# Attention and two expert layers on one core: weights of the second layer decoded once into float32, and the last block's products in another order

## The chip, the cores and the metric

The kernel runs on one core of one Trainium2 chip. The metric is the time of one execution on the device in microseconds; three runs of the kernel before are given, and one more execution was recorded by the hardware profiler.

## What is computed

The reference, cut to its core (shapes: 8 batches, 8 heads, 576 positions, head size 64; so 4608 tokens of width 512):

```
scores = q_c @ k_c.T / sqrt(64)              # in chunks of 64 positions
attn   = softmax(scores)
x      = (attn @ v_c)  as [4608, 512]
a, b   = x @ w1, x @ w2                       # [512, 1024] each
x      = ((a * b) @ w3) @ w_out               # [1024, 1024], [1024, 512]
h      = x @ w_in                             # [512, 2048]
out    = (h * cos(h)) @ w_out2                # [2048, 512]
```

The weights arrive as float64, each word pair of which the kernel turns into one float32 by itself.

## The kernel before, in words

The tokens are cut into 9 blocks of 512. Three kinds of matmul work follow each other for a block: attention (four tiles of 128 tokens, lines 724 to 787), the products a and b (ab, line 1000), and u, the product with w3 @ w_out folded into one matrix (lines 1110 to 1112). u is written to DRAM (line 1124). When all blocks are through, a second phase reads u back block by block and does h = u @ w_in (line 1318), cosine, and y = g @ w_out (line 1418). Every product of ab, h and y is a Strassen-Winograd product of seven terms on halves; each float32 operand is split into two float16 parts, so a term is three matmuls per piece. Three PSUM banks, x, y and z, collect the seven terms: ACT copies a bank out (`kept`), DVE adds another bank to what was copied (`plus`), and a term that continues in a bank (`more`) waits until the copy before it has been made.

Nothing in this kernel is issued in the order of the source. Each operation is recorded with an engine, a cost and a due time, and the class `Plan` lists them: at each moment every engine takes the waiting operation with the earliest due time whose buffers are free. The due times come from one line of constants (line 300). A2 and A3 set when the four attention tiles of a block are due ahead of its ab, I0 to I5 when the weights of the second layer are prepared, and Y0, Y1, YU when the terms of y and their weights are due. All loads and stores but one kind go through SP's queue, which is in order: an entry that waits holds up what stands behind it. The exception are additions of h operands by POOL's accumulating DMA (line 1348).

The second layer's weights are prepared while the blocks' ab and u run. `survey` (w_in first, w_out later) loads 16 pieces of 128 x 512 float64 each and takes the largest magnitude of each by a DVE reduction (line 584). From the maximum comes a power-of-two scale (`scale_of`). Then `convert_in` and `convert_out` load the same pieces a second time. `decoded` turns each into float32 in place (one ACT operation, line 1166; three on DVE, lines 1169, 1172, 1175), which leaves the values in every second word. Sums and differences for the Strassen terms are made in the words between (line 1246 on DVE or POOL for w_in, line 1202 on DVE for w_out). Each operand is split in two float16 parts by ACT (lines 1261, 1218) and DVE (lines 1264, 1221) and stored to `win_dram` and `wout_dram` (lines 1267, 1225). The second phase fetches them from there for every block (lines 1275, 1283).

`y_of` for the last block uses banks x, y, z as for every other: terms 0 (x), 1 (y), 5 (z), 4 (x), 3 (x), 2 with weight 6 (z), and 6 with weight 2 (x). The last store to the output is line 1445.

Of the kernel before, what the change touches and what calls it, by code (L numbers as in the profile page):

```python
# [262 lines left out]
def fused_kernel(  # L263
# [36 lines left out]
    R0, R1, C0, C1, A0, A1, A2, A3, R2, RL, C2, W0, X0, I0, I1, I2, I3, I4, I5, F0, Y1, Y0, YU = 2.0, 9.7, 15.9, 27.4, 89.8, 11.4, 70.0, 10.6, 47.7, 4.0, 74.1, -0.1, 14.0, 260.0, 10.0, 28.1, 410.0, 5.6, 11.6, 8.4, 16.0, 8.0, 9.05  # L300
# [79 lines left out]
    )  # L380
    two_p = sbuf_pool(one_half, *line("CONV", 24 * KB, 2 * KB, 4))
# [80 lines left out]
    with tc.manual_schedule():  # L462
# [619 lines left out]
        def u_scales(first, last, prio):  # L1082
# [4 lines left out]
            (b, t), c = small([P, 3, m], f"hsc{first}"), 2.0 ** (TOP - 2) / DM  # L1087
# [70 lines left out]
        def decoded(at, j, n, pool):  # L1158

            raw = load_raw(at, piece_of(j, n), "raw", pool)  # L1160
            def low():
                return raw.ap[:, :, 0]
            def high():
                return raw.ap[:, :, 1]
            def f():
                nc.scalar.activation(high().bitcast(F32), high().bitcast(F32), AF.Copy, scale=2.0**-112)
            op("ACT", 0.67, at - 2, f, r=[raw], w=[(raw, 1)])
            def f():
                nc.vector.tensor_scalar(low(), low(), 29, None, ALU.logical_shift_right)
# [12 lines left out]
        def convert_out(prio, step):
# [8 lines left out]
            def side(raw, n, h):  # L1191
                return raw.ap[:, 256 * h : 256 * h + 256, n].bitcast(F32)

            for kt in range(8):
                at = prio + 2 * step * kt
                top, low = (decoded(at + i * step, 1, kt + 8 * i, raw2_p) for i in range(2))
                at += step
                b11, b12, b21, b22 = ((raw, 0, h) for raw in (top, low) for h in range(2))
                t1, t3, t2, t4 = ((raw, 1, h) for raw in (top, low) for h in range(2))
# [8 lines left out]
                for i, (raw, n, os, m) in enumerate(((top, 0, slice(0, 1), 0), (low, 0, slice(1, 3), 0), (top, 1, slice(3, 6, 2), 0), (low, 1, slice(4, 7, 2), 1))):  # L1208
# [6 lines left out]
                    def val(raw=raw, n=n, width=width):  # L1215
                        return raw.ap[:, :width, n].bitcast(F32).rearrange("p (o e) -> p o e", e=256)
# [317 lines left out]
```

## Time and profile before

| what | us |
|---|---|
| runs of the kernel before, median (lowest to highest of 3) | 1413.06 (1412.48 to 1414.01) |
| the profiled execution, own time | 1407.62 |
| its span, first to last instruction | 1405.4 |
| PE busy in the span | 1367.8 (97%) |
| DVE, ACT, POOL busy | 1169.8, 961.3, 233.4 |

The page shows for each engine the time in which an instruction of it ran. PE is TensorE's matmuls. Idle time of PE is put down to the engine whose semaphore came last. The granted clock of TensorE is at its upper level, 2.4 GHz, from 50 to 1400 us.

### The profile page before, as it was taken

Reading aid. Unit: us, or ns where it says so; the run is one execution under the profiler, and the core shown is the slowest. Engines: PE = TensorE matmul, PEld = TensorE weight load, DVE = VectorE, ACT = ScalarE, POOL = GpSimd, SP = SyncE. Lnnn points to the kernel's source line nnn. Section 1 sums busy time; section 2 is a strip of 40 time slices with the busy share of each in tenths; the row PEclk is TensorE's granted clock in tenths of the full one; section 3 lists DMA queues with packets and bytes.
Section 4 is the critical chain, followed back from the end, with each engine's and each line's share of the span. In section 5 each row is a group of like instructions: output and inputs, shape, how many; then the busy total and the mean of one; then the engine's idle time right before and its main releaser. Section 6 shows DMA issues by size and latency. Waiting matters only on the chain.

```text
span 1405.4 us, 32143 instructions
## 1 busy us (share of the span) xinstructions
PE 1367.8 (97%) x12984; PEld 1103.3 (79%) x12984; DVE 1169.8 (83%) x2014; ACT 961.3 (68%) x2098; POOL 233.4 (17%) x198
## 2 busy tenths in 40 slices
PE   8889999999999999999999999999999999999998
PEld 5447677868676777786877888888888888888887
DVE  7999887448897878984669999999999898988883
ACT  5987786769886769885557666675656565755651
POOL 0000124113643212332111010000010011010000
PEclk9999999999999999999999999999999999999999
DMA  9962582236669528541625888778887878787634
GB/s 286 307 142 46 168 275 52 71 76 175 162 182 294 167 69 233 158 135 31 241 76 175 260 245 274 261 243 260 267 255 233 286 244 269 241 267 240 239 124 148
DMA packets 196628, 276.81 MB, mean 197 GB/s; under 512 B 121216, under 2 KB 151936, under 8 KB 187264
## 3 DMA queue, kind: packets, MB, share of 16 engines
q1 hardware_dynamic: 187264, 257.99, 57.5%
q0 software_dynamic: 9216, 16.78, 6.8%
q8 instruction: 101, 1.65, 0.5%
q14 instruction: 47, 0.39, 0.1%
HBM read 224.40 MB, written 33.55 MB: 184 GB/s over the span
## 4 chain that ended last, share of the span: by engine, by line
PE 71%; DVE 17%; DMA 5%; ACT 4%; issue 2%; SPq 1%; ACTq 0%; DVEq 0%; POOLq 0%
PE ps L1000 19%; PE ps L1418 18%; PE ps L1318 16%; PE ps L1110 4%; PE ps L1112 4%; PE ps L1111 4%; DVE W L1342 3%; DVE RES L1361 2%; DMA WG<-in_moe_w_dram 2%; PE ps L724 2%; PE ps L787 1%; PE ps L739 1%; DVE RES L1358 1%; DMA ATT<-in_v_dram 1%; DVE W L896 1%
## 5 line engine op out<-in xcount | busy, mean ns | idle before, releaser
L1000 PE MATMUL ps<-XHL,W 128*128 128x256 f16 x3024 | 349.2, 273 | 6.6 <-ACT RES L490 4.2
L1318 PEld LDWEIGHTS <-ATT 128*128 128x128 f16 x3024 | 295.7, 98 | 42.7 <-issue 6.9
L1000 PEld LDWEIGHTS <-W 128*128 128x128 f16 x3024 | 292.3, 98 | 46.8 <-issue 8.7
L1418 PE MATMUL ps<-CONV,W 128*128 128x256 f16 x2352 | 278.0, 273 | 1.7 <-ACT CONV L1433 1.6
L1418 PEld LDWEIGHTS <-W 128*128 128x128 f16 x2352 | 230.0, 98 | 29.2 <-issue 2.2
L1318 PE MATMUL ps<-XHL,ATT 128*128 128x256 f16 x1536 | 190.6, 273 | 2.1 <-DVE XHL L667 1.5
L1364 ACT ACTIVATE RES<-RES,quarter 128x512 f32<-128x512 f32 x144 | 103.4, 718 | 99.8 <-DVE RES L1361 99.5
L490 ACT ACTIVATE RES<-ps,smalls 128x512 f32<-128x512 f32 x126 | 86.7, 696 | 44.8 <-PE ps L1000 41.6
L1020 DVE SCALAR_TENSOR_TENSOR RES<-ps,smalls,RES 128x512 f32<-128x512 f32 x108 | 79.6, 745 | 41.3 <-ACT RES L490 27.3
L1110 PE MATMUL ps<-WG 128*128 128x512 f16 x288 | 109.3, 379 | 0.2 <-DVE RES L1070 0.2
L1112 PE MATMUL ps<-WG 128*128 128x512 f16 x288 | 109.2, 379 | 0.0
L1111 PE MATMUL ps<-WG 128*128 128x512 f16 x288 | 109.2, 379 | 0.0
L1035 POOL TENSOR_TENSOR WG<-RES,WG 128x512 f16<-128x512 f32 x49 | 63.0, 1291 | 271.1 <-ACT WG L486 271.0
L756 ACT ACTIVATE ATT<-ps,SMALL 128x64 f32<-128x64 f32 x288 | 85.7, 326 | 29.2 <-DVE SMALL L751 24.1
L1318 PE MATMUL ps<-WG,ATT 128*128 128x256 f16 x768 | 94.1, 273 | 1.2 <-DVE WG L1333 0.4
L1318 PE MATMUL ps<-RES,ATT 128*128 128x256 f16 x720 | 89.1, 273 | 2.4 <-ACT WG L1327 2.4
L1339 ACT ACTIVATE W<-WG,smalls 128x512 f16<-128x512 f32 x102 | 71.8, 714 | 22.7 <-DVE WG L1352 9.7
L1418 PE MATMUL ps<-CONV,WG 128*128 128x256 f16 x672 | 81.7, 273 | 0.0
L1342 DVE SCALAR_TENSOR_TENSOR W<-WG,smalls,W 128x512 f16<-128x512 f32 x102 | 74.8, 746 | 2.6 <-ACT W L1339 2.4
L667 DVE SCALAR_TENSOR_TENSOR XHL<-XHL,smalls 128x512 f16<-128x512 f32 x80 | 65.3, 838 | 10.7 <-ACT XHL L664 10.5
L486 ACT COPY ATT<-ps 128x512 f32<-128x512 f32 x108 | 61.3, 593 | 18.6 <-PE ps L724 9.6
L1348 POOL DMA_DIRECT2D WG<-WG x30 | 26.8, 893 | 277.7 <-DVE WG L1352 84.1
(211 smaller groups left out, 2395.8 us busy)
## 6 DMA issues: line engine op xcount, KB each, us to landing
ATT<-win_dram SPq DMA_DIRECT2D x72, 896.0 KB, 6.9
CONV<-wout_dram SPq DMA_DIRECT2D x63, 1024.0 KB, 6.1
CONV<-in_moe_w_in_dram SPq DMA_DIRECT2D x32, 512.0 KB, 6.2
CONV<-in_moe_w_out_dram SPq DMA_DIRECT2D x32, 512.0 KB, 6.1
ATT<-in_v_dram SPq DMA_DIRECT2D x144, 64.0 KB, 3.1
u_dram<-TMP SPq DMA_DIRECT2D x36, 256.0 KB, 3.7
XHL<-u_dram SPq DMA_DIRECT2D x9, 1024.0 KB, 8.2
out_dram<-CONV SPq DMA_DIRECT2D x36, 256.0 KB, 5.4
```

What stands on the lines that cost most here:

```text
L490: nc.scalar.activation(dst, src, AF.Copy, scale=s)
L756: nc.scalar.activation(probs()[:, b, a], scores()[:, a, b], AF.Exp, scale=scale, bias=mb.ap[:, 1, a, b : b + 1], accum_out=zb.ap[:, b, a : ...
L1000: nc.tensor.matmul(ps.ap[:, p * half : (p + 1) * half], w12[j, g].ap[:, b, w_, c, p * P : (p + 1) * P], t[a].ap[:, c, u_], start=(not more ...
L1020: nc.vector.scalar_tensor_tensor(b.ap, ps.ap, inv[1], b.ap, ALU.mult, ALU.add)
L1110: nc.tensor.matmul(ps.ap, wh.ap[:, kk, 0, ns], g[:, 0], start=(kk == 0), stop=False)
L1111: nc.tensor.matmul(ps.ap, wh.ap[:, kk, 0, ns], g[:, 1], start=False, stop=False)
L1112: nc.tensor.matmul(ps.ap, wh.ap[:, kk, 1, ns], g[:, 0], start=False, stop=(kk == K1 - 1))
L1318: nc.tensor.matmul(ps.ap[:, p * half : (p + 1) * half], wins[p].ap[:, b, k, w_], t[a].ap[:, k, u_], start=(not more and p == 0 and k == 0 ...
L1339: nc.scalar.activation(d.ap[:, 0], hs.ap, AF.Copy, scale=sg[1])
L1342: nc.vector.scalar_tensor_tensor(d.ap[:, 1], hs.ap, sg[1], d.ap[:, 0], ALU.mult, ALU.subtract)
L1364: nc.scalar.activation(r.ap, r.ap, AF.Sin, bias=quarters[side], scale=(2 * side - 1) * TURN)
L1418: nc.tensor.matmul(ps.ap[:, j * 256 : (j + 1) * 256], g[:, u_, n, j * P : (j + 1) * P], w.ap[:, 2 * f_ + n, w_], start=(not more and f_ == ...
```

## The change

Five things are done. `survey` decodes each piece, once, into float32, takes the sum of its squares on ACT instead of a maximum on DVE, and stores the 256 KB to a new DRAM tensor `dec_dram`; the scale comes from the sum (`sum_of`, `root_of`). `decoded` now only loads 256 KB of float32 from there. The differences for w_in are made in place, on DVE alone, and their operands read adjacent words. The last block's terms run in the order 0, 1, 5, 4, 2, 3, 6, where term 2 goes to bank y and term 6 to two banks of h, one for each half of its rows, each half added and stored by itself. And constants change: A2, A3, I0, I2, I3, I4, Y0, Y1, YU (F0 is read nowhere).

```diff
-    R0, R1, C0, C1, A0, A1, A2, A3, R2, RL, C2, W0, X0, I0, I1, I2, I3, I4, I5, F0, Y1, Y0, YU = 2.0, 9.7, 15.9, 27.4, 89.8, 11.4, 70.0, 10.6, 47.7, 4.0, 74.1, -0.1, 14.0, 260.0, 10.0, 28.1, 410.0, 5.6, 11.6, 8.4, 16.0, 8.0, 9.05
+    R0, R1, C0, C1, A0, A1, A2, A3, R2, RL, C2, W0, X0, I0, I1, I2, I3, I4, I5, F0, Y1, Y0, YU = 2.0, 9.7, 15.9, 27.4, 89.8, 11.4, 65.0, 7.2, 47.7, 4.0, 74.1, -0.1, 14.0, 241.9, 10.0, 34.8, 416.4, 5.7, 11.6, 7.2, 16.4, 10.3, 8.8
...
+    dec_p = sbuf_pool(plain, *line("CONV", 24 * KB, 2 * KB, 4))
+    piece_p = sbuf_pool(plain, *line("CONV", 0, 2 * KB, 12), queue=True)
...
-            (b, t), c = small([P, 3, m], f"hsc{first}"), 2.0 ** (TOP - 2) / DM
+            (b, t), c = small([P, 3, m], f"hsc{first}"), 2.0 ** (TOP - 2)
...
+        dec_dram = dram.tile([2, 16, P, 512], F32, name="dec_dram")
+        kept_f = Buf(None, "dec_dram")
+
         def survey(j, prio, step):
 
-            pm = small([P, 16], f"pmi{j}")
+            pm = small([P, 1, 16], f"pmi{j}")
             for n in range(16):
-                raw = load_raw(prio + step * n, piece_of(j, n), "look", raw2_p)
-                def f(raw=raw, n=n):
-                    absmax(pm[1][:, n : n + 1], raw.ap[:, :, 1].bitcast(F32))
-                op("DVE", 0.69, prio + step * n, f, r=[raw], w=[(pm[0], n)])
-            b, t = small([P, 16], f"wm{j}")
-            def f():
-                nc.vector.tensor_scalar(t, pm[1], 2.0**-112, None, ALU.mult)
-                nc.vector.tensor_scalar(t.bitcast(U32), t.bitcast(U32), 3, None, ALU.logical_shift_left)
-            op("DVE", 0.35, prio + 16 * step, f, r=[(pm[0], n) for n in range(16)], w=[b])
-            wsc[j] = scale_of(prio + 16 * step, b, t, f"wio{j}")
+                at = prio + step * n
+                raw, c = load_raw(at, piece_of(j, n), "raw", raw2_p), Buf(dec_p, f"dec{j}_{n}")
+                def low(raw=raw):
+                    return raw.ap[:, :, 0]
+                def high(raw=raw):
+                    return raw.ap[:, :, 1]
+                def f(high=high):
+                    nc.scalar.activation(high().bitcast(F32), high().bitcast(F32), AF.Copy, scale=2.0**-112)
+                op("ACT", 0.67, at - 2, f, r=[raw], w=[(raw, 1)])
+                def f(low=low):
+                    nc.vector.tensor_scalar(low(), low(), 29, None, ALU.logical_shift_right)
+                op("DVE", 0.45, at, f, r=[(raw, 0)], w=[(raw, 0)])
+                def f(low=low, high=high):
+                    nc.vector.scalar_tensor_tensor(low(), high(), 3, low(), ALU.logical_shift_left, ALU.bitwise_or)
+                op("DVE", 0.78, at, f, r=[(raw, 0), (raw, 1)], w=[(raw, 0)])
+                def f(low=low, high=high, c=c):
+                    nc.vector.scalar_tensor_tensor(c.ap.bitcast(U32), high(), SIGN, low(), ALU.bitwise_and, ALU.bitwise_or)
+                op("DVE", 0.7, at, f, r=[(raw, 1), (raw, 0)], w=[c])
+                def f(c=c, n=n):
+                    squares(pm[1][:, 0, n : n + 1], junk, c.ap)
+                op("ACT", 0.7, at + 1, f, r=[c], w=[(pm[0], n)])
+                def f(c=c, n=n):
+                    nc.sync.dma_start(dec_dram[j, n], c.ap)
+                op("SP", 0.6, at + 1, f, r=[c], w=[(kept_f, (j, n))], size=P * 2 * KB)
+            q = sum_of(prio + 16 * step, pm[0], range(16), pm[1], f"wm{j}")
+            wsc[j] = root_of(prio + 16 * step, *q, f"wio{j}")
...
         def decoded(at, j, n, pool):
+            raw = Buf(pool, f"piece{j}_{n}")
+            def f():
+                nc.sync.dma_start(raw.ap, dec_dram[j, n])
+            op("SP", 0.6, at - 10, f, r=[(kept_f, (j, n))], w=[raw], size=P * 2 * KB)
...
+                        def f():
+                            nc.vector.tensor_tensor(out=value(out), in0=value(x), in1=value(y), op=ALU.subtract)
+                        op("DVE", 0.7, at, f, r=[x, y, out], w=[out])
+                    def goes(o, raw, i):
+                        four_parts(at + i * step / 14, raw, (fb, fs), o, k, c)
+                    goes(0, b11, 0)
+                    sub(b12, b11, b11)
+                    sub(b22, b12, b12)
+                    goes(2, b22, 1)
+                    goes(1, b21, 2)
+                    sub(b22, b11, b22)
+                    goes(3, b11, 3)
+                    sub(b21, b22, b21)
+                    goes(5, b12, 4)
+                    goes(4, b22, 5)
+                    goes(6, b21, 6)
...
+            if last:
+                m4 = Buf(ps_y["y"], "psy4")
+                m3 = [Buf(ps_h, f"psy3_{j}") for j in range(2)]
+                multiply(x, 4, 4, 3, True)
+                c21 = kept(x, "u2", 3)
+                plus(z, c21, 3)
+                multiply(m4, 2, 6, 4)
+                plus(m4, c21, 4)
+                store(c21, 1, 0, 4)
+                multiply(x, 3, 3, 5, True)
+                c22, c12 = kept(x, "v5", 5), kept(x, "v3", 5)
+                plus(z, c22, 5)
+                store(c22, 1, 1, 5)
+                w = fetch(bl, 2, prio + 6 * unit - Y1)
+                for j in range(2):
+                    def f(j=j):
+                        for f_ in range(4):
+                            g = tg[6, f_].ap.rearrange("p s (f t) -> p s f t", f=2)
+                            for n in range(2):
+                                for m, (u_, w_) in enumerate(((0, 0), (1, 0), (0, 1))):
+                                    nc.tensor.matmul(
+                                        m3[j].ap[:, :256], g[:, u_, n, j * P : (j + 1) * P], w.ap[:, 2 * f_ + n, w_],
+                                        start=(f_ == 0 and n == 0 and m == 0), stop=(f_ == 3 and n == 1 and m == 2),
+                                    )
+                    op("PE", 12 * MM, prio + 6 * unit + j, f, r=[tg[6, f_] for f_ in range(4)] + [w], w=[m3[j]])
+                    def f(j=j):
+                        nc.vector.scalar_tensor_tensor(c12.ap[:, j], m3[j].ap[:, :256], iy[1], c12.ap[:, j], ALU.mult, ALU.add)
+                    op("DVE", 0.4, prio + 6 * unit + j, f, r=[m3[j], iy[0], c12], w=[(c12, j)])
+                    def f(j=j):
+                        nc.sync.dma_start(out[bl * T + j * P : bl * T + (j + 1) * P, 256:], c12.ap[:, j])
+                    op("SP", 0.6, prio + 6 * unit + j, f, r=[(c12, j)], size=P * KB)
+                return
```

The order of the instructions follows from the plan, so here are two places of it. Line numbers in the changed kernel are higher: L1138 is the raw load L1136 of before, L1126 the store of u, L642 and L719 the loads of v and of q and k.

SP's queue where the survey of w_in begins, before:

```order
L640 DMA ATT<-in_v_dram 64x4x64 x4
L717 DMA ATT<-in_k_dram 128x8x64
L1136 DMA CONV<-in_moe_w_in_dram 128x1024 x12
L1124 DMA u_dram<-TMP 128x512
L640 DMA ATT<-in_v_dram 64x4x64 x4
L1136 DMA CONV<-in_moe_w_in_dram 128x1024 x4
L1124 DMA u_dram<-TMP 128x512 x2
```

and from the middle of that survey on in the changed kernel (L1174 is the new store):

```order
L719 DMA ATT<-in_k_dram 128x8x64
L1138 DMA CONV<-in_moe_w_in_dram 128x1024
L1174 DMA dec_dram<-CONV 128x512
L1138 DMA CONV<-in_moe_w_in_dram 128x1024
L1126 DMA u_dram<-TMP 128x512
L1138 DMA CONV<-in_moe_w_in_dram 128x1024
L1174 DMA dec_dram<-CONV 128x512 x2
L1126 DMA u_dram<-TMP 128x512 x2
L1138 DMA CONV<-in_moe_w_in_dram 128x1024
L1174 DMA dec_dram<-CONV 128x512
```

The burst of raw loads is gone; loads now alternate with stores that wait for DVE, and the stores of u stand among them.

DVE's last rows, before (L1439 is `plus`):

```order
L1342 SCALAR_TENSOR_TENSOR WG<-RES,smalls,WG 128x512
L1342 SCALAR_TENSOR_TENSOR W_67<-W_67,smalls 128x512 x3
L1439 SCALAR_TENSOR_TENSOR CONV<-ps_77,smalls,CONV 128x512
L1439 SCALAR_TENSOR_TENSOR CONV<-ps_78,smalls,CONV 128x512 x2
```

and in the changed kernel (L1457 is `plus`, L1498 the addition of one half):

```order
L1457 SCALAR_TENSOR_TENSOR CONV<-ps_78,smalls,CONV 128x512
L1457 SCALAR_TENSOR_TENSOR CONV<-ps_77,smalls,CONV 128x512
L1457 SCALAR_TENSOR_TENSOR CONV<-ps_78,smalls,CONV 128x512
L1498 SCALAR_TENSOR_TENSOR CONV<-ps_76,smalls,CONV 128x256
L1498 SCALAR_TENSOR_TENSOR CONV<-ps_75,smalls,CONV 128x256
```

The last work behind PE moves from ACT's copy of a whole bank to DVE's addition of a half.

## Rows read from the trace of the kernel before

**Rows 1.** The page of the whole kernel: span, and busy time of each engine
```profile
span 1405.4 us, 32143 instructions
PE 1367.8 (97%) x12984; PEld 1103.3 (79%) x12984; DVE 1169.8 (83%) x2014; ACT 961.3 (68%) x2098; POOL 233.4 (17%) x198
```

**Rows 2.** Windows by stage: busy us (instructions) of each engine, granted clock, DMA share, GB/s
```profile
325.00:425.00 100.00, 97.99 (x1053) 77.22 (x1053) 91.01 (x131) 85.28 (x231) 51.80 (x34) 1.00 0.63 171
425.00:500.00 75.00, 71.70 (x789) 53.70 (x787) 58.38 (x109) 54.45 (x153) 23.34 (x19) 1.00 0.73 222
650.00:725.00 75.00, 74.26 (x604) 53.66 (x603) 42.49 (x77) 36.79 (x77) 14.33 (x10) 1.00 0.33 122
725.00:800.00 75.00, 72.98 (x619) 59.99 (x617) 71.05 (x126) 54.16 (x88) 7.19 (x8) 1.00 0.65 200
800.00:875.00 75.00, 74.19 (x678) 66.01 (x676) 73.94 (x122) 48.26 (x76) 7.73 (x9) 1.00 0.85 276
875.00:950.00 75.00, 71.98 (x658) 64.06 (x656) 72.14 (x119) 49.21 (x77) 6.11 (x7) 1.00 0.78 247
950.00:1375.00 425.00, 425.00 (x3896) 380.87 (x3894) 384.33 (x623) 259.41 (x398) 36.23 (x40) 1.00 0.77 243
```

**Rows 3.** Waits of PE, 375 to 500 us: total us, times, longest us
```profile
PE ps L1000 <- ACT RES L490: 3.0, 2, 1.5
PE ps L739 <- ACT ATT L756: 1.4, 1, 1.4
```

**Rows 4.** Waits of PE, 640 to 930 us
```profile
PE ps L1318 <- ACT WG L1327: 2.7, 2, 2.4
PE ps L1318 <- DVE XHL L667: 1.5, 1, 1.5
PE ps L1318 <- DVE WG L1333: 1.1, 2, 0.7
```

**Rows 5.** Waits of ACT, 888 to 927 us
```profile
ACT W L1339 <- DMA RES<-W: 3.2, 1, 3.2
```

**Rows 6.** Timeline of the end: start us, us, instruction [idle before, releaser]
```profile
1384.02 0.69 ACT L1433 ACTIVATE CONV<-ps,smalls 128x512 f32<-128x512 f32 x1 [6.79 <-PE ps L1418]
1384.76 5.40 PE L1418 MATMUL ps<-CONV,W 128*128 128x256 f16 x48 [0.78 <-ACT CONV L1433]
1390.93 10.64 PE L1418 MATMUL ps<-CONV,W 128*128 128x256 f16 x96 [0.78 <-ACT CONV L1433]
1401.66 0.69 ACT L1433 ACTIVATE CONV<-ps,smalls 128x512 f32<-128x512 f32 x1 [10.78 <-PE ps L1418]
```

**Rows 7.** DMA issues, 1401 to 1406 us: KB each, median us from issue to landing
```profile
out_dram<-CONV SPq DMA_DIRECT2D x1, 256.0 KB, 2.1
```

**Rows 8.** Groups of instructions by form: busy us, mean ns | idle before
```profile
L570 ACT ACTIVATE junk<-XHL 128x512 bf16<-128x512 f32 x36 | 22.7, 630 | 1.1
L570 ACT ACTIVATION_READ_ACCUMULATOR junk<-XHL 128x1 f32 x36 | 6.7, 186 | 0.0
L584 DVE TENSOR_REDUCE smalls<-CONV 128x1 f32<-128x512 f32 x32 | 21.2, 681 | 12.3 <-DMA CONV<-in_moe_w_out_dram 11.7 <-DMA CONV<-in_moe_w_in_dram 0.6
L1172 DVE SCALAR_TENSOR_TENSOR CONV<-CONV 128x512 uint32<-128x512 uint32 x32 | 31.6, 987 | 1.4
L1367 DVE TENSOR_TENSOR WG<-WG,RES 128x512 f32<-128x512 f32 x76 | 51.9, 685 | 4.9 <-ACT RES L1364 4.7
L1202 DVE TENSOR_TENSOR CONV<-CONV 128x256 f32<-128x256 f32 x32 | 14.8, 483 | 0.2
L1246 POOL TENSOR_TENSOR CONV<-CONV 128x512 f32<-128x512 f32 x13 | 22.5, 1733 | 15.7 <-DVE CONV L1175 12.7 <-DVE SMALL L763 1.4 <-PE ps L724 1.3
```

**Rows 9.** DMA issues of the whole kernel, from the page
```profile
CONV<-in_moe_w_in_dram SPq DMA_DIRECT2D x32, 512.0 KB, 6.2
```

**Rows 10.** Waits of SP's DMA queue, 170 to 700 us
```profile
SPq L1267 <- DVE CONV L1264: 25.6, 12, 7.2
```

**Rows 11.** Waits of PE, 0 to 100 us
```profile
PE ps L724 <- DMA ATT<-in_q_dram: 2.5, 1, 2.5
```

More of the change, by code (lines that the diff above doesn't have):

```diff
@@ L1182, in convert_out, with value @@
+        def value(raw):
+            return raw.ap
         def convert_out(prio, step):
@@ L1189, in convert_out, with halves, side @@
             op("DVE", 0.3, prio, f, r=[bs], w=[fb])
-            def side(raw, n, h):
-                return raw.ap[:, 256 * h : 256 * h + 256, n].bitcast(F32)
+            def halves(raw, width):
+                return [(raw, h) for h in range(width // 256)]
+            def side(raw, h):
+                return raw.ap[:, 256 * h : 256 * h + 256]
             for kt in range(8):
                 at = prio + 2 * step * kt
-                top, low = (decoded(at + i * step, 1, kt + 8 * i, raw2_p) for i in range(2))
+                top, low = (decoded(at + i * step, 1, kt + 8 * i, piece_p) for i in range(2))
                 at += step
-                b11, b12, b21, b22 = ((raw, 0, h) for raw in (top, low) for h in range(2))
-                t1, t3, t2, t4 = ((raw, 1, h) for raw in (top, low) for h in range(2))
+                more = [Buf(piece_p, f"sums{kt}_{i}") for i in range(2)]
+                b11, b12, b21, b22 = ((raw, h) for raw in (top, low) for h in range(2))
+                t1, t3, t2, t4 = ((raw, h) for raw in more for h in range(2))
                 def sub(x, y, out, how=ALU.subtract):
@@ L1202, in f @@
                         nc.vector.tensor_tensor(out=side(*out), in0=side(*x), in1=side(*y), op=how)
-                    op("DVE", 0.4, at, f, r=[x[:2], y[:2]], w=[out[:2]])
+                    op("DVE", 0.4, at, f, r=[x, y], w=[out])
                 sub(b11, b12, t1)
@@ L1207, in convert_out @@
                 sub(b21, t2, t4)
-                for i, (raw, n, os, m) in enumerate(((top, 0, slice(0, 1), 0), (low, 0, slice(1, 3), 0), (top, 1, slice(3, 6, 2), 0), (low, 1, slice(4, 7, 2), 1))):
+                for i, (raw, os, m) in enumerate(((top, slice(0, 1), 0), (low, slice(1, 3), 0), (more[0], slice(3, 6, 2), 0), (more[1], slice(4, 7, 2), 1))):
                     dst, width = Buf(two4_p, f"wo{kt}_{i}"), 256 if i == 0 else 512
@@ L1240, in convert_in, with four_parts @@
                     at = prio + step * (2 * k + c)
-                    b11, b12, b21, b22 = (decoded(at + i * step / 8, 0, 4 * (k + 2 * (i // 2)) + c + 2 * (i % 2), raw2_p) for i in range(4))
+                    b11, b12, b21, b22 = (decoded(at + i * step / 8, 0, 4 * (k + 2 * (i // 2)) + c + 2 * (i % 2), piece_p) for i in range(4))
                     at += step / 2
                     def sub(x, y, out):
-                        def f(eng):
-                            engines[eng].tensor_tensor(out=value(out, 1), in0=value(*x), in1=value(*y), op=ALU.subtract)
-                        op(TT, 0, at, f, r=[x, y], w=[(out, 1)])
-                    sub((b12, 0), (b11, 0), b11)
-                    sub((b22, 0), (b11, 1), b22)
-                    sub((b22, 0), (b12, 0), b12)
-                    sub((b21, 0), (b22, 1), b21)
-                    for o, (raw, n) in enumerate(((b11, 0), (b21, 0), (b22, 0), (b11, 1), (b22, 1), (b12, 1), (b21, 1))):
-                        four_parts(at + o * step / 14, raw, n, (fb, fs), o, k, c)
-        def four_parts(at, raw, n, scale, o, k, c):
+                        def f():
[14 more added lines that the diff above has]
+                    goes(6, b21, 6)
+        def four_parts(at, raw, scale, o, k, c):
             dst = Buf(two4_p, f"wi{o}_{k}{c}")
```

36 lines of the change are left out of this document (9 added, 27 removed).

## Prediction

> **What bounds the kernel.** I read the page first: PE is busy in 1367.8 of 1405.4 us [rows 1], so all that any change of order can give back is the 37.6 us in which PE stood idle. The number of matmuls hardly changes (two small transposes and their followers go, two small sums come), so a gain must come out of idle time, and the windows by stage tell where that lies. From 325 to 500 us PE lacks 2.01 and 3.30 us, from 650 to 725 us 0.74, and in the first part of the second phase, 725 to 950 us, 2.02, 0.81 and 3.02 us [rows 2]. From 950 to 1375 us nothing is lost: 425.00 of 425.00 [rows 2]. So the long second phase cannot be made faster by this change at all, whatever it does to other engines there. These six windows hold 11.9 us and the end 5.4 (below); the other 20.3 us lie elsewhere, nearly all ahead of 325 us, where the first weights are made and the change leaves the work alone.
>
> The waits of PE then say what ended the idle time. From 375 to 500 us it is ACT: 3.0 us for the copy out of a bank (L490) and 1.4 us for an exponential of attention (L756) [rows 3]. From 640 to 930 us it is again ACT's copy (2.7 us), the float16 parts of u (1.5 us) and `plus` (1.1 us) [rows 4]. The largest of these, 2.4 us, comes after ACT has stood 3.2 us at the head of its queue for an accumulating DMA that landed late [rows 4, 5]. At the end there are two waits of 0.78 us each for a copy of bank x, and after the last matmul (1390.93 + 10.64 = 1401.57 us) another 3.83 us until the span ends [rows 6].
>
> **The last block's terms.** Before, term 3 is added in bank x directly behind term 4, so PE waits 0.78 us for the copy, and the next term waits 0.78 us for the copy of term 3 [rows 6]. Now term 2 goes to bank y and stands between terms 4 and 3; it takes 48 matmuls, which last 5.40 us, and the copy it hides lasts 0.69 us [rows 6]. Term 6 goes to two banks of h that nothing uses any more, so nothing is waited for there either. Both waits go: **-1.56 us**. If the cover were gone, the same 0.78 us each would be back; no third wait is late next, since the last weights have two whole terms, some 10.6 us, to land [rows 6].
>
> **The last store.** Before, ACT copies a bank of 128 x 512 in 0.69 us [rows 6], and 256 KB need 2.1 us from issue to landing [rows 7]. Now DVE adds 128 x 256; the nearest row of that size took 483 ns [rows 8]: -0.2 us. The store has 128 KB left. Its landing lies between 2.1 us (no gain) and half of that, 1.05 us; no row has this size at an idle queue. I take 1.7 us, -0.4, since part of a landing is there for any size. Together **-0.6 us**, with ends of -0.2 and -1.25. [...]
>
> **Preparing w_in and w_out.** What goes on DVE: 32 maxima of 681 ns, 21.8 us [rows 8]. The three decoding operations per piece are moved to the survey, not removed. What comes on ACT: 32 squares at 630 ns and, behind each, a read of the accumulator at 186 ns, 20.2 us at least and 26.1 us if nothing overlaps [rows 8]. POOL loses its 13 differences, 22.5 us at 1733 ns each, and DVE takes them at some 685 ns, +8.9 us [rows 8]. One decoding operation took 987 ns on average where a float32 operation of the same size takes 685 ns [rows 8]; with POOL off these tiles and the converting reads adjacent, up to 0.3 us of each such operation may go, 9.7 us for 32. So DVE loses 12.9 to 22.6 us and ACT gains 20 to 26 us.
>
> In bytes nothing changes: 32 second loads of 512 KB (half of the 32 of w_in [rows 9] and as many of w_out) make 16.8 MB, and 32 stores and 32 loads of 256 KB make 16.8 MB. But SP issues 32 entries more, and each store waits for DVE.
>
> All of this lies beside PE's work, so by itself I cost it at nothing. The cover on ACT is its idle time: it is busy 85.28 of 100 us from 325 to 425, and 54.45 of 75 us from 425 to 500 [rows 2]; one survey adds 10 to 13 us, which would fill the fuller window to about 98. If that cover goes, the copies out of the banks come late, and PE pays as in [rows 3]. DVE at 91.01 of 100 us [rows 2] gets lighter, though, and ACT's exponentials and copies wait on DVE's operations about as often as the reverse.
>
> **The constants.** A block's last attention tile is due at 70 - 3 x 10.6 = 38.2 us ahead of its ab before, and at 65 - 3 x 7.2 = 43.4 us now: 5.2 us more lead for the operands of ab, and the tiles closer together. Both waits of [rows 3] stand where a block's ab begins while exponentials of the next tiles fill ACT's queue. I take half of the 5.31 + 0.74 us of these stages [rows 2] as saved: **-3.0 us**. The ends are -6.05 (all of it) and +6 (as much again, if ACT's added squares do there what the exponentials do now).
>
> For the second phase Y0 + i x YU moves term 0 by +2.3 us and term 6 by +0.8 us, with weights asked for 0.4 us earlier. This shuffles which operation stands in front of which between 725 and 950 us, where DVE is busy 71 to 74 of 75 us [rows 2] and has no slack to repair a late DMA. There 5.85 us are lost, about half of it behind one late landing [rows 5]. An order that is another one need not repeat it, and may have its own: I take **-1.0 us**, between -5.85 and +3.0 (one more such landing).
>
> **The sum.** -1.56 - 0.6 - 3.0 - 1.0 = -6.2 us. The profiled execution took 1407.62 us by its own time, 2.2 more than its span, and would come to 1401.4. The runs shown have a median of 1413.06, 0.4% above the profiled one; the difference goes onto the median: 1406.9 us.
>
> **Rivals.** *Only the end is gained.* The plan deals out the same PE work against nearly the same sums of other engines; a wait removed at one block's start can reappear at another's. Then -1.56 - 0.6 is what is left, 1410.9 us. For it speaks that PE's idle time in the middle stages is only 6.05 us in all, so that little noise eats a part of it; against it, that both ends of the tiles' schedule move the right way.
>
> *All idle time of these stages goes.* -2.2 - 6.05 - 5.85 = -14.1, or 1399.0 us. Against it: six stages would have to be clean where each lost something before [rows 2].
>
> *SP's queue holds up attention: slower.* The 32 added stores each wait on SP until DVE has decoded a piece. Stores of the like (L1267) were held 25.6 us over 12 waits, 2.1 us each, 7.2 at most [rows 10]. Behind them in the queue stand loads of q, k, v and the stores of u, as the order of SP's rows shows. Loads of q and k are asked for 12 units ahead of use (line 717), so the rival decides once about six mean holds fall in a row. PE's price for one late load of q was 2.5 us [rows 11]; at three blocks' starts that is +7.5, with the end -2.2: +5.3, or 1418.4 us. Against it: the loads in the burst that was there before are gone, and in the survey's windows DMA is busy 0.63 to 0.73 of the time [rows 2]. The Trainium skill's page "DMA: Bandwidth & Descriptors", section "Anatomy of one DMA", says that DMA engines do not wait for semaphores and that the issuing sequencer does so before dispatch; by that rule a held store delays all that SP issues later, and the trace agrees: SP's own waits are listed as such [rows 10].
>
> *The change doesn't do what it says.* If pieces were still read as float64 the second time, nothing would move in the stage. The order shows loads of 128 x 512 from `dec_dram`, so this has 0.02, at 1413.
>
> **How the numbers follow.** A measurement of this kernel can tell about 0.2%, 2.8 us, from no change. Forecast (-3 to -10): 0.48. All goes: 0.10. Only the end, -2.2, inside 0.2%: 0.25. No effect: 0.02. Slower: 0.15. So faster by over 0.2% 0.58, within 0.27, slower 0.15. The range reaches from 1400.0 (the forecast's -6.2 with most of the remaining idle time gone) to 1414.5 (only the end, with a new wait of some 3.6 us); outside are half of the second rival and nearly all of the slower one, some 0.18.
>
> **What would show it.** In the changed kernel's trace: no wait of PE for L1433's successor in the last block, and under 3.5 us from the last matmul to the end; no maxima on DVE, 32 squares on ACT; PE's waits for ACT's copies between 200 and 725 us at about 3 us in all; some 5 us of idle PE from 725 to 950 us. It would be wrong if PE's waits name q, k or v loads or ACT's copies for over 6 us between 200 and 725 us, or if the start of the second phase loses as much as before or more.

## The result, and the profile after

| what | before | after |
|---|---|---|
| median of 4 runs, us (lowest to highest) | 1412.77 (1411.77 to 1414.01) | 1401.35 (1400.49 to 1401.85) |
| ratio of the runs, 95% interval | | 0.9918 [0.9901, 0.9935] |
| recorded execution, own time and span, us | 1407.62, 1405.4 | 1401.22, 1398.8 |

The change saves 11.4 us by the medians, but only 6.4 us between the two recorded executions. Before was recorded 5.2 us below its median, after 0.1 us. That gap makes up nearly half of the saving.

The changed kernel's page, for [rows 1]:

```profile
span 1398.8 us, 32260 instructions
PE 1365.6 (98%) x12977; PEld 1102.3 (79%) x12982; DVE 1153.0 (82%) x1994; ACT 974.4 (70%) x2162; POOL 206.5 (15%) x183
```

DVE lost 16.8 us, ACT gained 13.1 and POOL lost 26.9. PE's idle time fell from 37.6 to 33.2 us. The windows by stage of the changed kernel (busy us and instructions of PE, weight loads, DVE, ACT, POOL; granted clock, DMA share, GB/s), for [rows 2]:

```profile
325.00:425.00 100.00, 96.14 (x1062) 75.47 (x1060) 86.27 (x140) 87.05 (x237) 33.73 (x25) 1.00 0.84 244
425.00:500.00 75.00, 75.00 (x822) 57.19 (x821) 48.13 (x93) 56.50 (x172) 16.22 (x13) 1.00 0.36 98
650.00:725.00 75.00, 75.00 (x613) 54.60 (x612) 44.55 (x76) 34.69 (x62) 16.69 (x12) 1.00 0.29 108
725.00:800.00 75.00, 72.95 (x619) 60.10 (x617) 71.25 (x126) 54.58 (x89) 7.22 (x8) 1.00 0.65 200
800.00:875.00 75.00, 74.31 (x680) 66.30 (x678) 74.21 (x124) 49.75 (x78) 8.08 (x9) 1.00 0.85 271
875.00:950.00 75.00, 74.69 (x685) 66.77 (x684) 71.79 (x117) 49.44 (x78) 7.24 (x8) 1.00 0.79 255
950.00:1375.00 425.00, 425.00 (x3895) 380.94 (x3894) 387.63 (x628) 257.67 (x397) 34.88 (x39) 1.00 0.75 243
```

From 425 to 500 us nothing is lost any more (3.30 before), from 875 to 950 us 0.31 (3.02 before). From 325 to 425 us the loss grew from 2.01 to 3.86 us, at a DMA share of 0.84 where it was 0.63. PE's waits of the changed kernel from 640 to 930 us (total us, times, longest), for [rows 4]:

```profile
PE ps L1336 <- DVE XHL L669: 1.4, 1, 1.4
PE ps L1336 <- DVE WG L1351: 1.0, 2, 0.7
PE ps L1336 <- ACT WG L1345: 0.4, 1, 0.4
PE ps L1336 <- DMA ATT<-win_dram: 0.3, 1, 0.3
```

The 2.7 us behind ACT's copy are down to 0.4. The end of the changed kernel's timeline (start us, us, instruction, idle before), for [rows 6]:

```profile
1375.80 14.14 PE L1436 MATMUL ps<-CONV,W 128*128 128x256 f16 x128
...
1389.77 5.40 PE L1492 MATMUL ps<-CONV,W 128*128 128x256 f16 x48
1389.97 1.27 ACT L1451 ACTIVATE CONV<-ps,smalls 128x512 f32<-128x512 f32 x2 [9.79 <-PE ps L1436]
...
1395.21 0.48 DVE L1498 SCALAR_TENSOR_TENSOR CONV<-ps,smalls,CONV 128x256 f32<-128x256 f32 x1 [2.07 <-PE ps L1492]
```

No row of PE has an idle time before it: both waits of 0.78 us are gone. The last matmul ends at 1395.17 us, 3.63 us ahead of the span's end (3.83 before). The groups by form that answer to [rows 8]:

```profile
L572 ACT ACTIVATE junk<-CONV 128x512 bf16<-128x512 f32 x32 | 20.8, 650 | 0.6 <-DVE CONV L1168 0.3
L572 ACT ACTIVATION_READ_ACCUMULATOR junk<-CONV 128x1 f32 x32 | 6.9, 215 | 0.0
L1168 DVE SCALAR_TENSOR_TENSOR CONV<-CONV 128x512 uint32<-128x512 uint32 x32 | 29.5, 922 | 0.6
L1213 DVE TENSOR_TENSOR CONV<-CONV 128x256 f32<-128x256 f32 x32 | 18.9, 625 | 0.2
L1257 DVE TENSOR_TENSOR CONV<-CONV 128x512 f32<-128x512 f32 x16 | 13.3, 831 | 0.3
```

The squares cost 27.7 us on ACT. A decoding operation fell from 987 to 922 ns. The sums of w_out rose from 483 to 625 ns each; in e9, where they read the same words as before, they take 651 ns, so the new layout needn't be the cause. The 16 differences on DVE take 831 ns each.

### The profile page after: what moved, and what is told of

Its sections match the earlier page's. It is cut to its first block, busy times and chain, and to the rows that moved or that the text cites. A ratio compares the mean times of both kernels' runs of the same rounds, so it can differ in the third digit from the quotient of the medians.

```text
span 1398.8 us, 32260 instructions
## 1 busy us (share of the span) xinstructions
PE 1365.6 (98%) x12977; PEld 1102.3 (79%) x12982; DVE 1153.0 (82%) x1994; ACT 974.4 (70%) x2162; POOL 206.5 (15%) x183
## 4 chain that ended last, share of the span: by engine, by line
PE 74%; DVE 15%; ACT 4%; DMA 4%; issue 2%; SPq 1%; POOL 0%; ACTq 0%; DVEq 0%
PE ps L1002 20%; PE ps L1436 19%; PE ps L1336 17%; PE ps L1112 4%; PE ps L1113 4%; PE ps L1114 4%; DVE W L1360 3%; PE ps L726 2%; PE ps L950 2%; DVE RES L1379 1%; PE ps L789 1%; PE ps L741 1%; DVE RES L1376 1%; DMA CONV<-in_moe_w_out_dram 1%; DVE XHL L669 1%
## 5 line engine op out<-in xcount | busy, mean ns | idle before, releaser
L1436 PE MATMUL ps<-CONV,W 128*128 128x256 f16 x2304 | 273.4, 273 | 0.0
L1357 ACT ACTIVATE W<-WG,smalls 128x512 f16<-128x512 f32 x101 | 71.3, 713 | 25.0 <-DVE WG L1385 12.6
L1345 ACT ACTIVATE WG<-ps,smalls 128x512 f32<-128x512 f32 x76 | 51.0, 680 | 48.5 <-PE ps L1336 47.9
L669 DVE SCALAR_TENSOR_TENSOR XHL<-XHL,smalls 128x512 f16<-128x512 f32 x81 | 68.5, 863 | 9.0 <-ACT XHL L666 8.9
L1360 DVE SCALAR_TENSOR_TENSOR W<-WG,smalls,W 128x512 f16<-128x512 f32 x101 | 74.1, 745 | 0.9 <-ACT W L1357 0.8
L1436 PEld LDWEIGHTS <-WG 128*128 128x128 f16 x672 | 65.8, 98 | 7.6
```

The source lines that it names most:

```text
L669: nc.vector.scalar_tensor_tensor(d.ap[:, :, 1], ap(x), scale[1], d.ap[:, :, 0], ALU.mult, ALU.subtract)
L1360: nc.vector.scalar_tensor_tensor(d.ap[:, 1], hs.ap, sg[1], d.ap[:, 0], ALU.mult, ALU.subtract)
L1436: nc.tensor.matmul(ps.ap[:, j * 256 : (j + 1) * 256], g[:, u_, n, j * P : (j + 1) * P], w.ap[:, 2 * f_ + n, w_], start=(not more and f_ == ...
```

## The experiments

The idle time below is worked out from each kernel's windows by stage: the width less PE's busy time. L584 waits are DVE's waits for raw pieces at the survey's maxima from 425 to 500 us. The last column is the time from 200 to 1375 us in which the granted clock stood at its lower level, 1.2 GHz. PE counts as busy there, but its matmuls start at half the rate (e1's rows below), so up to half of that time is lost on top of the idle time. One execution of each kernel was recorded, so a microsecond between two rows can be chance; the ratios come from 4 to 12 runs each, and e1 to e4, e5 to e8 and e9 to e12 ran on one chip each, beside runs of before.

| kernel | ratio to before [95%] | PE idle 200 to 725 | 725 to 950 | 950 to 1375 | L584 waits | at 1.2 GHz |
|---|---|---|---|---|---|---|
| before | 1 | 6.05 | 5.85 | 0 | 11.7 | 0 |
| e1, before again | 1.0002 [0.9991, 1.0014] | 7.31 | 5.30 | 0.85 | 13.1 | 6.8 |
| e2, last block only | 0.9984 [0.9971, 0.9997] | 7.60 | 4.24 | 1.57 | 12.5 | 0 |
| e3, constants only | 0.9945 [0.9927, 0.9963] | 4.00 | 3.73 | 0 | 5.4 | 6.8 |
| e4, decoding only | 0.9945 [0.9929, 0.9962] | 4.14 | 4.47 | 0 | none | 6.8 |
| after | 0.9918 [0.9901, 0.9935] | 4.42 | 3.05 | 0 | none | 0 |
| e5, after, old A2, A3 | 0.9960 [0.9946, 0.9974] | 3.54 | 6.62 | 0.35 | none | 3.4 |
| e6, after, old Y | 0.9945 [0.9925, 0.9964] | 2.94 | 4.73 | 0 | none | 0 |
| e7, after, old I | 0.9919 [0.9905, 0.9934] | 2.27 | 3.19 | 0.51 | none | 0 |
| e8, after, nudged | 0.9940 [0.9921, 0.9960] | 3.43 | 4.66 | 0 | none | 0 |
| e9, before, no survey of w_out | 0.9963 [0.9948, 0.9977] | 7.10 | 3.77 | 0 | none | 3.4 |
| e10, after, squares twice | 0.9899 [0.9882, 0.9916] | 4.50 | 3.99 | 0 | none | 0 |
| e11, after, one last store | 0.9912 [0.9897, 0.9928] | 3.60 | 3.06 | 0.09 | none | 0 |
| e12, after, later surveys | 0.9894 [0.9876, 0.9912] | 3.05 | 3.14 | 0.26 | none | 3.4 |

### The kernel before once more, and each part alone

**Before again** has no edit; it shows how two recordings of one program differ.

> The kernel before, unchanged, with a profile of its own. The recorded execution of before took 1407.6 us while its other runs took 1411.8 to 1414.0; the changed kernel's recorded execution (1401.2) lies among its other runs. Theory A (the trace that I read shows before as it mostly runs): a new recorded execution comes out within 2 us of 1407.6 again or of 1412.8, and shows the same idle stretches of PE. Theory B (before has a wait whose length varies from run to run, by some 5 us, which the trace I read had at its short end): a new trace shows one or two idle stretches of PE that are longer than in the first, most likely at a late accumulating DMA or a late load between 375 and 925 us, with the rest equal.

It was recorded at 1414.96 us, 7.3 us above the first recording, as Theory B had it: PE has a longer wait behind late loads. DVE's timeline of this second recording:

```profile
440.20 0.69 DVE L584 TENSOR_REDUCE smalls<-CONV 128x1 f32<-128x512 f32 x1 [2.68 <-DMA CONV<-in_moe_w_out_dram]
...
447.27 0.69 DVE L584 TENSOR_REDUCE smalls<-CONV 128x1 f32<-128x512 f32 x1 [0.61 <-DMA CONV<-in_moe_w_out_dram]
448.63 0.69 DVE L584 TENSOR_REDUCE smalls<-CONV 128x1 f32<-128x512 f32 x1 [0.67 <-DMA CONV<-in_moe_w_out_dram]
450.03 0.74 DVE L1070 SCALAR_TENSOR_TENSOR RES<-ps,smalls,RES 128x512 f32<-128x512 f32 x1
```

and what PE waited for there, from 425 to 500 us:

```profile
PE ps L1110 <- DVE RES L1070: 2.1, 1, 2.1
PE ps L739 <- ACT ATT L756: 1.3, 1, 1.3
PE ps L1000 <- DVE XHL L667: 0.3, 1, 0.3
```

Each maximum stands at the head of DVE's in-order queue until its 512 KB have landed. L1070, which empties a bank of PE, comes behind them; so PE waits 2.1 us for the bank. In the first recording L1070 ran at 445.51 us and the same wait was 0.2 us; in e2's, which has the same survey, it was 1.6 us. The wait has a sequel, in PE's timeline:

```profile
450.83 0.38 PE L1110 MATMUL ps<-WG 128*128 128x512 f16 x1 [2.11 <-DVE RES L1070]
...
452.39 0.63 PE L1110 MATMUL ps<-WG 128*128 128x512 f16 x1
452.82 0.63 PE L1111 MATMUL ps<-WG 128*128 128x512 f16 x1
...
455.97 0.38 PE L1111 MATMUL ps<-WG 128*128 128x512 f16 x1
456.18 0.38 PE L1112 MATMUL ps<-WG 128*128 128x512 f16 x1
```

and in the windows:

```profile
451.80:455.20 3.40, 3.40 (x10) 1.21 (x8) 2.77 (x9) 3.01 (x11) 2.44 (x3) 0.50 0.94 259
```

From 451.8 to 455.2 us the granted clock is 0.50, the lower level, and the matmuls start every 0.43 us instead of every 0.21: 1.7 us are lost that no column of idle time shows. The same happens from 926.3 to 929.7 us, behind a wait of 2.34 us. A late landing at 1252.84 us (ACT idle 3.02 us) cost PE 0.9 us more.

The two spans differ by 6.5 us (1411.9 and 1405.4; the other 0.8 lies outside the span). When the first block's ab begins, e1 is already 2.0 us behind (97.5 against 95.5 us), before any of the second layer's weights are loaded (from 159 us on); at 254 us it is 1.6. When the first h begins it is 4.7 us behind (723.3 against 718.6), at the last block's h 6.5 (1296.0 against 1289.5). Of the 3.1 us between 254 and 723 us, idle time is 1.3 (7.31 less 6.05) and the lower clock 1.7. So two executions of one program differ by late transfers with an engine waiting for them at the head of its queue, by stretches at the lower clock behind PE's waits, and by the start of the kernel.

**The last block alone.**

```diff
-            multiply(x, 3, 3, 4, True)
+            multiply(m4, 2, 6, 4)
...
```

> Before, with only the last block's new order of terms and halved last term. Theory A: the two waits of 0.78 us go and nothing else, so 1.6 to 2.2 us less than before, ratio 0.9985. Rival: the plan re-sorts the work of the last two blocks around the new terms and a new wait eats it, ratio 1.000 or more.

Measured 1410.45 us against 1412.96 of e1 in the same series: -2.5 us, by the ratio -0.16% [-0.29, -0.03]. The forecast's two terms for the end stand at -2.2.

**The constants alone, and the decoding alone.**

```diff
-... A2, A3, ... = ... 70.0, 10.6, ... I0 260.0, I2 28.1, I3 410.0, I4 5.6, Y1 16.0, Y0 8.0, YU 9.05
+... A2, A3, ... = ... 65.0, 7.2, ... I0 241.9, I2 34.8, I3 416.4, I4 5.7, Y1 16.4, Y0 10.3, YU 8.8
```

> Before, with only the new constants. Theory A (the lead and spacing of attention carry the middle stages): 3 to 6 us less than before, ratio 0.996 to 0.998. Rival (the constants are fitted to the decoded-once survey and do nothing or harm with the old one): ratio 1.000 to 1.004.

```diff
-                raw = load_raw(prio + step * n, piece_of(j, n), "look", raw2_p)
...
+                    nc.sync.dma_start(dec_dram[j, n], c.ap)
```

> Before, with only the pieces decoded once (old constants, old last block). Theory A: DVE 13 to 22 us lighter and ACT 20 us heavier beside a PE that is full, so within 2 us of before. Rival C (the burst of 512 KB loads in the surveys is what makes before's loads of v and stores of u late, and decoding once removes it): 4 to 8 us less, ratio 0.994 to 0.997. Rival D (ACT's squares and SP's waiting stores make attention late): 3 to 6 us more.

Each alone saves 0.55%, some 7.8 us, more than Theory A of either had. So the decoding alone is worth as much as the constants alone, and the parts don't add: 0.16 + 0.55 + 0.55 = 1.26% alone, 0.82% together. The table suggests that either removes some of what the other would have: L584's waits fall to 5.4 us with the new constants alone and to none with the decoding, and PE's idle time from 200 to 725 us is 4.00, 4.14 and 4.42 us with the one, the other and both. That isn't shown, for the two lose in different places. e3 loses 3.23 us from 425 to 500 us, behind exponentials (L787 behind L756), with 6.8 us at 1.2 GHz after it. e4 loses nothing there, but 4.38 us from 725 to 800 us, again with 6.8 us at 1.2 GHz, where before and after lose 2.02 and 2.05.

Rival C came true by its size. Of its path the traces show a part: from 200 to 725 us ACT stood at the head of its queue for stores of u for 3.0, 4.4 and 3.6 us in before, e1 and e2, and not at all in e4; PE's waits behind that (L1121) were only 0.4 to 1.0 us. Rival D's 3 to 6 us more didn't come.

### Which constants

```diff
e5: A2, A3 = 70.0, 10.6 in place of 65.0, 7.2
e6: Y1, Y0, YU = 16.0, 8.0, 9.05 in place of 16.4, 10.3, 8.8
e7: I0, I2, I3, I4 = 260.0, 28.1, 410.0, 5.6 in place of 241.9, 34.8, 416.4, 5.7
e8: I2, Y0 = 34.3, 10.0 in place of 34.8, 10.3
```

> The changed kernel with A2 and A3 back at 70 and 10.6 (attention's lead and spacing). Theory A (the longer lead of the last tile removes waits at the start of a block's ab): 3 to 5 us more than the changed kernel, ratio to before 0.994 to 0.996, with waits of PE for ACT's bank copies from 425 to 500 us back. Rival (decoding once has removed that wait by itself, as in the run with decoding alone, where 425 to 500 us lost nothing): within 1.5 us of the changed kernel, ratio 0.991 to 0.993.

> The changed kernel with Y0, Y1, YU back at 8.0, 16.0, 9.05. Theory A (another order of y's terms avoids the late accumulating DMA near 903 us): 2 to 3 us more, ratio 0.993 to 0.995, with 2 to 3 us of idle PE from 875 to 950 us. Rival (that wait goes with anything that shifts the second phase, since decoding alone lost 0.09 us there): no change from 875 to 950 us, ratio 0.991 to 0.993.

> The changed kernel with I0, I2, I3, I4 back at 260, 28.1, 410, 5.6 (when the surveys and conversions are due). Theory A (they only follow the other parts): within 1.5 us of the changed kernel. Rival (they carry the gain of the middle stages): 3 us or more above it, ratio to before 0.994 or more.

> The changed kernel with I2 34.3 for 34.8 and Y0 10.0 for 10.3, changes too small to mean anything by themselves, which still re-sort the plan. It measures how much of any difference here is the luck of one order. Theory A (the parts carry the gain): within 1.5 us of the changed kernel, ratio to before 0.991 to 0.993. Rival (the constants were fitted to one order, and a neighbouring order is as good as any): 3 us or more above it, ratio 0.994 or more.

Without the attention constants the ratio is 0.9960 in place of 0.9918, some 5.9 us (4.6 by the medians). That is the time of Theory A, but not its sign: from 425 to 500 us e5 loses nothing. PE's waits of e5 from 725 to 800 us show where it does:

```profile
PE ps L1336 <- DVE RES L669: 2.7, 1, 2.7
PE ps L1436 <- DVE W L1360: 1.3, 1, 1.3
PE ps L1436 <- ACT W L1357: 0.9, 1, 0.9
```

These rows, of u's parts (L669) and of operands of y (L1360, L1357), stand with the decoding alone too (2.1, 1.3 and 1.0 us); after has 1.4 us of the first and none of the others. With them e5 loses 4.90 us in place of 2.05, and 3.4 us at 1.2 GHz follow: together some 4.5 us, as much as the medians differ. Before and e3, with the old survey of w_out, lose only 2.02 and 2.12 us there. So the new A2 and A3 remove a wait that stands beside the decoding; e5 doesn't show what they save on the kernel before.

Old Y costs about 3.8 us by the ratios, with overlapping intervals; its runs scatter from 1400.42 to 1408.4 us, and 875 to 950 us loses 1.82 us in place of 0.31. But the nudge, half a unit and less, costs nearly as much: 1402.63 us (1401.43 to 1407.77), a ratio of 0.9940, and 1.57 us lost from 875 to 950. e5 loses 1.72 us there with the new Y, e4 0.09 with the old. So that wait doesn't hang on the values of Y, and the order that the numbers happen to make counts. Old I costs nothing, as Theory A had it. For the nudge itself the theories stay undecided: by the medians it is 1.3 us above after, within Theory A's 1.5, by the ratio it is at the rival's 0.994. Against this neighbour the attention constants are worth only 2.8 us by the ratios, with overlapping intervals.

### What the decoding removed

**No survey of w_out** leaves out the survey's 16 loads and 16 maxima; w_out takes w_in's scale.

```diff
-        survey(1, I3, I4)
+        wsc[1] = wsc[0]
```

> The kernel before without its survey of w_out: the 16 loads of 512 KB and the 16 maxima on DVE are left out, and w_out takes the scale of w_in. Theory A: the decoding gained because these maxima stood at the head of DVE's queue waiting for a burst of loads while PE's banks waited behind them. Then PE's idle time from 425 to 500 us (3.3 and 3.6 us in the two recordings of the kernel before) falls below 1 us, and the time falls by 2 to 4.5 us, a ratio of 0.997 to 0.9985 with less scatter. Rival: the waits there come from the blocks' starts (ACT's copies behind exponentials) and have nothing to do with the survey; then 3 us or more of idle time stay in that window and the ratio is within 0.999 to 1.001. DVE's busy time falls by 11 us either way.

Measured 1408.96 us against 1413.83, -4.9 us, a little more than Theory A had, and a range of 3.3 us over 5 runs against 5.0 over 9 of before. DVE's busy time fell by 6.0 us against the first recording and not by 11, mostly since the sums of w_out took 651 ns in place of 483. From 425 to 500 us PE lost 1.82 us, between the two theories' bounds, and its waits there are:

```profile
PE ps L1000 <- DVE XHL L667: 1.5, 1, 1.5
PE ps L1000 <- ACT RES L490: 0.3, 1, 0.3
```

L1070 and the exponential (L756) are gone from the list, so these waits hung on the survey, or on the order that it made; a wait at a block's start (L667) takes part of their place, so the blocks' starts matter as well. Taking out this one survey saves 4.9 of the 7.8 us that the decoding saves, but the trace doesn't place them: from 325 to 425 us e9 lost 3.62 us (before 2.01, e1 2.92), and from 725 to 800 us 3.77 with 3.4 us at 1.2 GHz behind them. The edit takes out 16 loads of 512 KB together with the maxima and re-sorts the plan, and no run leaves out one without the other; whether the maxima at the head of DVE's queue or the loads themselves cost most of it is open. The rest of the decoding's 7.8 us wasn't separated either (w_in's maxima, the burst of its loads, POOL's 13 differences).

**Squares twice.**

```diff
+                    squares(pm[1][:, 0, n : n + 1], junk, c.ap)
                     squares(pm[1][:, 0, n : n + 1], junk, c.ap)
```

> The changed kernel with every sum of squares of the survey made twice on ACT, 32 more activations and accumulator reads of some 0.8 us, 26 us more on ACT. Theory A, as the prediction priced it: ACT's idle time takes in the survey's added work, so doubling it costs under 1.5 us, a ratio to the kernel before of 0.991 to 0.993. Rival: ACT's copies out of the banks come late where the squares stand, PE waits for L488 in 200 to 500 us by 3 us or more beyond the changed kernel's, and the ratio is 0.994 or above.

The doubled group of e10:

```profile
L572 ACT ACTIVATE junk<-CONV 128x512 bf16<-128x512 f32 x64 | 40.8, 638 | 1.8 <-DVE smalls L579 0.6
L572 ACT ACTIVATION_READ_ACCUMULATOR junk<-CONV 128x1 f32 x64 | 12.7, 199 | 0.0
```

The group grew by 25.8 us, ACT's busy time as a whole by 18.9, since instructions overlap, and the time was 1400.53 us, not above after's. PE's waits for L488 from 200 to 500 us came to 2.3 us, 3.4 in the changed kernel. Theory A holds: ACT's idle time takes it in.

### The end, and an attempt at a better kernel

**One last store** in place of two.

```diff
-                    op("SP", 0.6, prio + 6 * unit + j, f, r=[(c12, j)], size=P * KB)
+                store(c12, 0, 1, 6)
```

> The changed kernel with the two halves of the last term stored by one transfer of 256 KB in place of two of 128 KB. By the prediction's term the halved store saves 0.4 us, so from the last matmul's end to the span's end this kernel should need 0.4 us more than the changed kernel's 3.63 us, about 4.0. Rival: a landing at an idle queue is nearly the same for both sizes, and the figure stays within 0.15 us of 3.63. The whole time can't tell them apart, the end of the timeline can.

The end of e11's timeline:

```profile
1394.83 1.26 PE L1492 MATMUL ps<-CONV,W 128*128 128x256 f16 x10
...
1396.13 0.48 DVE L1498 SCALAR_TENSOR_TENSOR CONV<-ps,smalls,CONV 128x256 f32<-128x256 f32 x1 [2.07 <-PE ps L1492]
1396.68 0.37 SPq L1463 DMA_DIRECT2D out_dram<-CONV  x1
```

The last matmul ends at 1396.09 us, 3.6 us ahead of the span's end at 1399.7: the rival holds. The store is issued 3.02 us ahead of the end; in the changed kernel it is

```profile
1395.72 0.34 SPq L1501 DMA_DIRECT2D out_dram<-CONV  x1
```

3.08 us. The landings do differ, after's last store first, e11's second:

```profile
out_dram<-CONV SPq DMA_DIRECT2D x1, 128.0 KB, 1.7
```

```profile
out_dram<-CONV SPq DMA_DIRECT2D x1, 256.0 KB, 2.1
```

but the 0.4 us between them don't reach the end of the span.

**Later surveys.**

```diff
-... I0 241.9, I2 34.8, I3 416.4, I4 5.7, I5 11.6
+... I0 260.0, I2 28.1, I3 424.0, I4 5.6, I5 11.0
```

> The changed kernel with the survey's and the conversion's due times moved later, w_in's to the value of before and w_out's to 424, so that the raw loads of w_out no longer fall together with the stores of w_in's operands at 325 to 425 us. Theory A: the 3.9 us of PE's idle time in that window are ACT waiting at the head of its queue for late raw loads; then the window falls below 2 us and the whole is 1 to 2 us faster than the changed kernel, a ratio to the kernel before of 0.9895 to 0.991. Rival: the waits move with the work, the idle time from 425 to 650 us grows by as much, and the ratio stays at 0.991 to 0.993 or rises because the first operands of h come late at 725 us.

From 325 to 425 us PE waited in the changed kernel for

```profile
PE ps L726 <- ACT ATT L488: 1.8, 1, 1.8
PE ps L789 <- ACT ATT L488: 1.6, 1, 1.6
```

and the first of these copies stood in ACT's queue behind a late raw piece:

```profile
413.81 0.67 ACT L1159 ACTIVATE CONV<-CONV 128x512 f32<-128x512 f32 x1 [1.27 <-DMA CONV<-in_moe_w_out_dram]
414.37 0.58 ACT L488 COPY ATT<-ps 128x512 f32<-128x512 f32 x1
```

The second stood behind operations of both stages (L1279, L1159) and a wait of 0.8 us for a store to `dec_dram`. ACT's waits there, in the changed kernel:

```profile
ACT CONV L1159 <- DMA CONV<-in_moe_w_out_dram: 3.9, 5, 1.6
ACT CONV L1279 <- DMA win_dram<-CONV: 2.9, 2, 1.7
```

and in e12:

```profile
ACT RES L492 <- PE ps L1002: 5.0, 5, 2.6
ACT TMP L492 <- DMA u_dram<-TMP: 3.3, 2, 2.8
...
ACT CONV L1159 <- DMA CONV<-in_moe_w_out_dram: 1.9, 1, 1.9
```

ACT's waits for raw pieces are halved, and PE loses 2.20 us there in place of 3.86, a little over the 2 us expected; 0.82 us of it comes back from 425 to 500 us. What is left from 325 to 425 us is one wait of 2.2 us behind the late store of u, with 3.4 us at 1.2 GHz after it. The median is 1399.15 us (1397.24 to 1402.38), the lowest of all, 2.3 us below e11 and 1.4 below e10 on the same chip. It beats the kernel before; that it beats the changed kernel isn't shown, as [0.9876, 0.9912] and [0.9901, 0.9935] overlap.

## Why the prediction was right, and where its steps were off

Faster by over 0.2% was forecast and measured, and 1401.35 us lies in the range, 5.6 us below the number. By its steps:

- **The last block's terms, -1.56.** Right. Neither wait is left, and e2 alone gave -2.5 us (0.03 to 0.29%) for both terms of the end.
- **The last store, -0.6.** Mis-sized: about 0.2 us, all of it the shorter last operation (DVE's 0.48 in place of ACT's 0.69). The landing of 1.7 us was as I took it, but the span ends about 3.0 us behind the issue for 128 KB as for 256 KB (e11). The sign named for it, under 3.5 us from the last matmul to the end, failed with 3.63. The Trainium skill's page "DMA: Bandwidth & Descriptors", section "Anatomy of one DMA", fits a fixed 2.0 us plus bytes at 436 GB/s to DMAs of the gpsimd path; by that the two landings would take 2.3 and 2.6 us, an estimate from that page. These stores go through SP's queue, and the rows' 1.7 and 2.1 decide.
- **The constants, -3.0 in the middle and -1.0 behind.** Recorded: 6.05 to 4.42, -1.6, and 5.85 to 3.05, -2.8; -4.4 in place of -4.0. That the sums meet is luck in part: the recording holds the decoding's effect as well, and the constants alone are worth some 7.8 us by the runs (e3). I had the attention tiles relieve the blocks' starts at 375 to 500 us. In e3 PE's waits for ACT's copies there do fall, from 3.0 to 0.4 us, but its waits for exponentials rise from 1.4 to 3.2; beside the decoding the earlier tiles pay at the start of the second phase (e5). At 325 to 425 us the loss rose, since raw loads of w_out now fall together with the stores of w_in's operands and ACT stands waiting for them (shown with e12); PE's waits for ACT's copies from 200 to 725 us came to 3.9 us, where I named about 3. The feared +6 from ACT's squares did not come, and twice the squares cost nothing either (e10).
- **Decoding once, at nothing.** Wrong as a price: alone it is worth some 7.8 us. I counted the engines' work, -12.9 to -22.6 us on DVE (measured -16.8) and +20 to +26 on ACT (the squares 27.7, ACT's busy time as a whole only 13.1), and looked for who covers it. What I left out was the place where DVE waited: I had quoted the 11.7 us that L584 stood waiting for w_out [rows 8] as a row and priced the 681 ns of the operation alone. e1 shows a bank of PE behind these waits (2.1 us, and 1.7 more by the clock), and without the survey of w_out 4.9 us go (e9). How the 7.8 us divide is open.
- **"The difference goes onto the median."** This is the step that cost the 5 us. The sum was made against the recorded 1407.62 us and came out right there: -6.2 forecast, -6.4 measured. But I carried before's 5.4 us between recording and median over unchanged, as if it belonged to the measurement. e1's recording shows what a slower execution of before has that the first one had not: 1.3 us more idle time and 1.7 us at the lower clock by the time the second phase begins, 1.8 us more behind that, and a start 1.6 us later. All 26 runs of before in the first series lie at 1409.9 us or above, so the first recording was a rare one and the sum rested on it. The changed kernel's recording is a typical one, 0.1 us from the median, and its 4 runs lie within 1.4 us. Which losses make up the whole gap is open, since of each kernel one or two executions were recorded.
- **The rivals.** SP's queue held the new stores 19.2 us over 15 waits in the changed kernel, 1.3 us each (L1174 behind DVE), but no wait of PE from 200 to 725 us names q, k or v: the slower rival's price was not paid. "All idle time goes" comes nearest by its number, 1399.0, but not as a mechanism: 7.5 us of idle time are still there from 200 to 950 us.

## What to carry to other kernels

When an operation is removed, price the wait ahead of it as well as its duration, and look at what stands behind it in the same in-order queue; an engine's wait for a transfer that nobody needs soon can hold up a bank that another engine needs now. Compare the recorded execution with the median first: where it lies several us below, those us are losses that its rows don't show, and the change may remove them too. Beside the idle time, look for stretches at the lower clock: the engine counts as busy there while its matmuls start at half the rate. The savings of parts needn't add, so the value of a part alone is not its share in the whole, and a neighbouring order of the same plan can differ by as much as a part.

## What was not expected of the hardware

The end of the span follows the issue of the last store by 3.0 to 3.1 us whether 128 or 256 KB are stored, though their landings differ by 0.4 us. What lies between the landing and the end no row shows.

A wait of PE can cost more than its length. Behind 200 us the recordings show seven stretches of 3.4 or 6.8 us at 1.2 GHz, and PE had just waited before or into each: 2.11 and 2.34 us in e1, 2.6 in e3, 0.96 and 1.28 in e4 (with 2.14 more inside the stretch), 0.86, 1.28 and 2.66 in e5, 2.12 in e9, 2.21 in e12. Such a wait doesn't always bring one: before's own wait of 2.35 us at 918.9 us was followed by none.

PE's listed busy time is no measure of its work to a few us: it ranges from 1365.6 us (after, mean granted clock 0.998) to 1370.6 (e1, 0.992) for nearly the same matmuls. The first 100 us of the changed kernel and of e12:

```profile
0.00:100.00 100.00, 81.31 (x539) 47.24 (x542) 84.06 (x159) 77.83 (x198) 0.78 (x8) 0.97 0.96 258
```

```profile
0.00:100.00 100.00, 83.32 (x536) 48.55 (x537) 82.69 (x157) 76.27 (x195) 0.78 (x8) 0.91 0.96 258
```

At a mean of 0.91 of 2.4 GHz in place of 0.97, three matmuls fewer are listed with 2 us more, in a stretch where PE idles 17 to 19 us for data anyway. So the mean clock of a whole execution doesn't tell its time: of after's four runs the fastest, 1400.49 us, had 0.994 and the slowest, 1401.85, 0.998. Where the clock is low while PE has no other wait, as in e1 from 451.8 to 455.2 us, it costs half of the stretch.
